# Moving small elementwise work off GpSimd in a chained attention and two-layer gated network kernel

## The chip, the cores and the metric

The kernel runs on one core of one Trainium2 chip. The metric is device time in microseconds (us), the median of several executions. A core has a matrix engine (TensorE, PE in the profile; its weight loads are PEld), VectorE (DVE), ScalarE (ACT), GpSimd (POOL) and SyncE (SP), which issues nearly all DMAs here. Each engine runs its own instructions in order.

## The reference

```python
scores = scale * (q @ k.T), causal            # q, k, v: 4 batches, 8 heads, 576 tokens, 64
local  = softmax(scores) @ v
q_p    = where(q > 0, q, exp(q) - 1) + 1
mem    = (q_p @ M_prev) / (q_p @ z_prev + 1e-6)
x      = g * mem + (1 - g) * local            # g = sigmoid(beta), per head; x: 2304 tokens x 512
xn     = x / rms(x) * rms_g
x      = (silu(xn @ w_gate) * (xn @ w_val)) @ w_out         # 512 -> 1536 -> 512
out    = (sigmoid(x @ w_gate2) * (x @ w_val2)) @ w_out2     # 512 -> 1536 -> 512
```

## The kernel before, in words

The work is cut into five **groups** of tokens. Group -1 holds the first 128 tokens of each of the four batches (512 tokens); groups 0 to 3 hold the other 448 tokens of one batch each. A group passes both gated layers, each in 12 **slices** of 128 hidden units: products with the gate and value weights (`pg`, `pv`, L1000), a tanh on ScalarE and two or three VectorE steps (`gated`), then the product with the output weights (`po`, L1066). While group g is in its layers, the attention of group g+1 is computed between its slices; so the program has an **opening** (attention of group -1 alone, written step by step in the string `ORDER`) and five stages.

Precision is kept by splitting each float32 operand into a high and a low half. For that, weights are scaled by a power of two found from a maximum. Group -1 does this for all weights, which arrive as 8-byte words: ScalarE and VectorE make float32 (`f64_top` L911, `f64_word` L917), `pair_sum` (L756) gives a sum of magnitudes per partition, `pair_scale` (L762) takes its maximum over partitions with GpSimd's `partition_all_reduce`, `two_power` (L740 to L746, VectorE) makes the scale and its inverse, ScalarE writes the scaled high half (L877) and VectorE the low half (L767). `pair_units` then lets GpSimd multiply the inverse with the token scale: `unit` and `kappa` (L775, L776) in layer 0, two columns (L778, L779) in layer 1. The tanh and the gating of the slice read those columns. The halves are saved to device memory, and later groups load them ready-made. The first two slices of layer 0 are prepared inside the opening (steps `wm`, `wp`, `wu`, `wh`, `wl` of `slice_stages`).

GpSimd's other work: maxima over partitions for the token scale `K` (L307), for values (L153), for the softmax (L597) and for the scale of the tokens between the layers (`xtop`, L1232); causal masks and fills; in the opening `phi_min` (L427), `av_add` (L420), `root` (L455) and once the scaling of `g_bc` (L1536); in the last group additions of halves for a Strassen-like product (`pair_load`, L1110) and a slice of units (L1401).

The order of the rest comes from a scheduler that places each step by priority, kept in bounds by tables, each indexed by group + 1: `DUE` (so many slices before the end of a stage the next group's attention has been dealt out), `HOLD` (the slice from which dealing starts), `AFTER` (how many slices a dealt step stays behind), `BACK` (the same for the weights of group -1), and `ONE` (between which slices of group 0 the output weights are rescaled). Weight tiles of group -1 come from a ring of six, two per slice.

Of the kernel before, what the change touches and what calls it, by code (L numbers as in the profile page):

```python
# [54 lines left out]
fill3 Aa1 W0 wp0 wu0 F0 fill3 U0 Ma2 Cb1 H0 Tb2 wt2 Vm1 Ab1 L0 fill2 S3 Va1 Xa2 Em3 Ph2 Ta2 Ph3 P2 Cb2
Ca2 Ma3 wh0 Y1 Q1 Mb3 Xa3 D2 N1 Ab2 Vm2 Aa2 wl0 Xb3 W1 fill1 P3 F1 Ta3 Ca3 U1 Tb3 Va2 D3 Vm3 Cb3 H1 wo2
Aa3 wt3 L1 Ab3 Va3 wo3 Y2 Q2 v0a g0a N2 wm1 Y3 Q3 wp1 W2 N3 F2 wh1 W3 U2 F3 wu1 a0a H2 U3 wl1 L2 H3
v1a g1a L3 dd0a a1a dd1a
# [8 lines left out]
def attn_moe_moe_kernel(ctx, tc, qT, kT, qk0, v, mz, beta, w8, rms_g, outT):  # L67
# [428 lines left out]
    def slice_stages(xt, ws, hs):  # L496

        do = {}
        for f in range(2):
# [372 lines left out]
    def halve(g, l, f, raw):  # L872
# [345 lines left out]
    def halve_tokens(g, n, po, xh):  # L1218
# [375 lines left out]
```

## Time and profile before

| | us |
|---|---|
| median of 3 executions | 1228.76 |
| lowest, highest | 1228.61, 1231.05 |
| the profiled execution: time | 1227.21 |
| the profiled execution: span of its instructions | 1225.4 |

| engine | busy us | share of the span |
|---|---|---|
| PE | 1036.7 | 85% |
| DVE | 821.2 | 67% |
| ACT | 619.3 | 51% |
| POOL | 250.4 | 20% |

The profile's busy time of an engine leaves out instructions that only set something up, so an idle time can be a wait for data or for such an instruction. In the profile's answers the idle time that an engine had before an instruction stands in brackets or behind a second bar, with what ended it; "issue" means that nothing in the profile ended it. The chain of waits is followed back from the last instruction.

### The profile page before, as it was taken

The page shows a single profiled execution, that of the slowest core. Times are in us where ns is not written, and L with a number is a line of the kernel's source. Part 1 is how long each engine was busy: PE and PEld are TensorE (multiplying, and loading weights), DVE is VectorE, ACT ScalarE, POOL GpSimd, SP SyncE. Part 2 cuts the span into 40 slices and gives each one's busy share as a digit, 9 for nine tenths or more (in the row PEclk, how much of TensorE's full clock was granted, in tenths as well). Part 3 has the DMA queues.
Part 4 walks back from the last instruction along what each step waited for, and adds up shares of the span by engine and source line. Part 5 has one row for each costly group of instructions (what it writes and reads, how often), then busy time and mean ns, then how long its engine had stood idle before and what let it go on. Part 6 is the DMA issues. An engine that isn't in the chain of part 4 may idle for free.

```text
span 1225.4 us, 18759 instructions
## 1 busy us (share of the span) xinstructions
PE 1036.7 (85%) x6721; PEld 661.7 (54%) x6721; DVE 821.2 (67%) x1730; ACT 619.3 (51%) x1078; POOL 250.4 (20%) x410
## 2 busy tenths in 40 slices
PE   4644666687658789999999999999999998799898
PEld 2532333455425446667665556655556654676675
DVE  2533446597456558888875978755878775886983
ACT  2534354568446547877553656543655542343343
POOL 2220011132112202233300312210322111330410
PEclk7778787888889899999999999999999998989999
DMA  6136464477536477886778783537644334534420
GB/s 239 53 111 243 152 206 170 153 268 259 179 138 232 160 219 259 293 259 234 253 243 259 243 273 114 179 119 225 206 150 124 129 112 108 177 129 147 147 91 36
DMA packets 90464, 223.28 MB, mean 182 GB/s; under 512 B 23938, under 2 KB 35714, under 8 KB 90370
## 3 DMA queue, kind: packets, MB, share of 16 engines
q1 hardware_dynamic: 90370, 222.08, 54.3%
q8 instruction: 53, 0.87, 0.3%
q14 instruction: 41, 0.34, 0.1%
HBM read 179.57 MB, written 38.80 MB: 178 GB/s over the span
## 4 chain that ended last, share of the span: by engine, by line
PE 51%; issue 17%; DVE 16%; ACT 7%; DMA 4%; POOL 4%; POOLq 0%; ACTq 0%; DVEq 0%
PE po L1066 14%; PE pg L1000 13%; PE pv L1000 12%; PE pw L1163 4%; PE ps L245 2%; DVE w L917 2%; ACT top L911 1%; POOL rd L1110 1%; DVE sw L1128 1%; DMA ha<-x 1%; DMA wr<-half 1%; PE pm L659 1%; DVE vl L172 1%; PE pav L610 1%; PE pav L612 1%
## 5 line engine op out<-in xcount | busy, mean ns | idle before, releaser
L1000 PEld LDWEIGHTS <-ws 128*128 128x128 f16 x1032 | 102.6, 102 | 135.3 <-issue 39.3
L1066 PE MATMUL po<-h,ws 128*128 128x448 f16 (+2 forms) x552 | 132.0, 383 | 11.8 <-DVE h L1038 6.2
L1020 ACT ACTIVATE t<-pg,unit 128x448 f32<-128x448 f32 (+2 forms) x92 | 58.5, 636 | 88.3 <-PE pg L1000 88.1
L578 POOL TENSOR_SCALAR_AFFINE_SELECT sc<-sc 128x128 f32<-128x128 f32 (+1 forms) x128 | 60.0, 484 | 155.8 <-ACT sc L573 155.2
L1000 PEld LDWEIGHTS <-wr 128*128 128x128 f16 x552 | 54.3, 99 | 61.3 <-issue 14.2
L1000 PEld LDWEIGHTS <-wl 128*128 128x128 f16 x408 | 40.1, 101 | 86.1 <-issue 23.3
L1066 PE MATMUL po<-h,wr 128*128 128x448 f16 (+1 forms) x384 | 85.1, 364 | 0.2 <-ACT h L1037 0.2
L1000 PE MATMUL pg<-ha,ws 128*128 128x448 f16 (+2 forms) x252 | 60.7, 394 | 21.2 <-DVE ws L767 11.7
L740 DVE TENSOR_SCALAR pw<-wtop 128x1 int32<-128x1 int32 x22 | 3.3, 149 | 111.5 <-POOL wtop L762 111.5
L597 POOL PARTITION_ALL_REDUCE mb<-mx x32 | 55.8, 1744 | 73.6 <-DVE mx L595 41.1
L245 PE MATMUL ps<-qq,kk 128*128 128x64 f16 (+2 forms) x280 | 54.7, 304 | 17.5 <-DVE s L746 8.1
L1066 PEld LDWEIGHTS po<-h,ws 128*128 128x128 f32 x300 | 56.4, 192 | 20.3 <-DVE h L1038 7.0
L1066 PE MATMUL po<-h,wl 128*128 128x448 f16 (+2 forms) x276 | 65.6, 381 | 0.0
L573 ACT COPY sc<-ps 128x512 f32<-128x512 f32 (+1 forms) x96 | 51.7, 559 | 20.4 <-PE ps L245 20.2
L1000 PE MATMUL pv<-hb,ws 128*128 128x448 f16 (+1 forms) x240 | 55.7, 381 | 6.5 <-DVE t L1029 4.5
L239 DVE TENSOR_TENSOR pt<-sc,pt 128x1472 f16<-128x1472 f32 x32 | 55.1, 1721 | 5.0 <-ACT pt L238 4.8
L1000 PE MATMUL pg<-hb,ws 128*128 128x448 f16 (+1 forms) x240 | 53.7, 366 | 2.0 <-ACT ws L877 1.1
L1000 PE MATMUL pv<-ha,ws 128*128 128x448 f16 (+2 forms) x252 | 54.4, 363 | 0.0
L598 DVE TENSOR_TENSOR sc<-sc,mb 128x896 f32<-128x896 f32 x32 | 34.7, 1085 | 28.3 <-POOL mb L597 28.3
L1029 DVE SCALAR_TENSOR_TENSOR t<-t,pv 128x448 f32<-128x448 f32 (+1 forms) x52 | 32.7, 629 | 28.8 <-PE pv L1000 25.1
L235 ACT ACTIVATE sc<-sc,qs 128x1472 f32<-128x1472 f32 x24 | 36.5, 1523 | 29.5 <-DVE sc L603 23.9
L1022 DVE SCALAR_TENSOR_TENSOR t<-t,pg 128x448 f32<-128x448 f32 (+2 forms) x50 | 30.8, 616 | 25.7 <-ACT t L1020 25.7
(364 smaller groups left out, 2642.2 us busy)
## 6 DMA issues: line engine op xcount, KB each, us to landing
raw<-in_w SPq DMA_DIRECT2D x22, 1023.8 KB, 5.5
ws<-half SPq DMA_DIRECT2D x34, 512.0 KB, 4.2
wr<-half SPq DMA_DIRECT2D x31, 512.0 KB, 4.3
rawl<-in_w SPq DMA_DIRECT2D x24, 511.8 KB, 6.3
wr<-parts SPq DMA_DIRECT2D x23, 512.0 KB, 5.9
ws<-parts SPq DMA_DIRECT2D x20, 512.0 KB, 5.0
kd<-in_kT SPq DMA_DIRECT2D x64, 144.0 KB, 3.7
parts<-ws SPq DMA_DIRECT2D x17, 512.0 KB, 2.9
```

The lines of the kernel that those rows point to most:

```text
L235: nc.scalar.activation(out=sc, in_=sc, func=AF.Exp, scale=both)
L239: nc.vector.tensor_tensor(out=pt[:, 1, 64:SW], in0=sc, in1=pt[:, 0, 64:SW], op=ALU.subtract)
L245: nc.tensor.matmul(ps[:, c0:c0 + n], kk[:, k0:k0 + 128], r[:, q0 - 128:q0 - 128 + n], start=(i == 0), stop=(i == 1))
L573: nc.scalar.copy(out=sc[:, o:o + c], in_=ps[:, 0:c])
L578: nc.gpsimd.affine_select(out=d, in_=d, compare_op=ALU.is_ge, fill=NEG, base=SQ[kt] - T0[kt], pattern=[[1, n]], channel_multiplier=-1,)
L597: nc.gpsimd.partition_all_reduce(mb[:, 0:448], mx[:, 0:448], channels=128, reduce_op=bass_isa.ReduceOp.max)
L598: nc.vector.tensor_tensor(out=two, in0=two, in1=mb[:, None, 0:448].to_broadcast([128, 2, 448]), op=ALU.subtract)
L1000: nc.tensor.matmul(ps[:, 0:n], w[:, a, k * 128:(k + 1) * 128], x[b][:, k, o:o + n], start=(i == 0), stop=(i == 3 * KD - 1))
L1020: nc.scalar.activation(out=t, in_=pg[:, 0:n], func=AF.Tanh, scale=u if half else 0.5)
L1029: nc.vector.scalar_tensor_tensor(out=t, in0=t, scalar=1.0, in1=pv[:, 0:n], op0=ALU.add, op1=ALU.mult)
L1066: nc.tensor.matmul(po[d][:, 0:n], w[2][:, a, c], hh[:, b, 0:n], start=(first and i == 0), stop=(last and i == 2))
L1163: nc.tensor.matmul(regions[m][at], left(i, m, a, k), right(j, b, k), start=first and c == 0, stop=c == 5, skip_group_check=True,)
```

## The change

GpSimd keeps its maxima over partitions and the masks. `pair_units` goes to ScalarE (two activations a slice in layer 0, one in layer 1, where the inverse is written straight into its column by VectorE), and so does the scaling of `g_bc`. Four maxima over partitions leave GpSimd: `K`, those of the two slices prepared in the opening, and the last group's `xtop`. In their place TensorE multiplies the column, spread over 128 columns, with the identity, and VectorE takes the maximum along the row (`widest`). `ORDER` gets two steps `wq` for that and sets `wp` and `wu` later; `K` comes first, and its load before the first load of queries and keys. The tables change.

```diff
-ONE = (1, 23, 5, 1)
-DUE = (5, 3, 3, 13, 8)
-HOLD = (1, 1, 1, 1, 1)
-BACK = (3,)
-AFTER = (1, 3, 3, 3)
+ONE = (1, 21, 6, 1)
+DUE = (6, 8, 4, 14, 8)
+HOLD = (1, 1, 1, 3, 1)
+BACK = (6,)
+AFTER = (2, 3, 2, 3)
...
-    LOADS = "q0 c q1 w0 v0 m0 b q2 v1 m1 g w1 v2 m2 q3 v3 m3 w2 w3"
+    LOADS = "c q0 q1 w0 v0 m0 b q2 v1 m1 g w1 v2 m2 q3 v3 m3 w2 w3"
...
-            top = ap_.tile([128, 1], F32, tag="gtop", name="gtop")
-            nc.gpsimd.partition_all_reduce(top, gm, channels=128, reduce_op=bass_isa.ReduceOp.max)
-            z["sx"], inv = two_power(top, 1, 7)
+            bank = zps.tile([128, 512], F32, tag="pm", name="pk")
+            z["sx"], inv = two_power(widest(gm, bank[:, 0:128])(), 1, 7)
...
+            def spread(f=f):
+                bank = z["pg", 0] if f else z["pm"][:, 0]
+                z["max", f] = widest(z["sum", f], bank[:, 384:512])
...
-                z["sw", f], z["isw", f] = pair_scale(z["sum", f])
+                z["sw", f], z["isw", f] = two_power(z["max", f](), 1, 12)
...
         if l == 0:
-            nc.gpsimd.tensor_scalar(out=unit[0][:, c], in0=inv, scalar1=half_isx, scalar2=None, op0=ALU.mult)
-            nc.gpsimd.tensor_tensor(out=kappa[:, c], in0=unit[0][:, c], in1=unit[0][:, c], op=ALU.mult)
+            nc.scalar.activation(out=unit[0][:, c], in_=inv, func=AF.Copy, scale=half_isx)
+            nc.scalar.activation(out=kappa[:, c], in_=inv, func=AF.Square, scale=half_isx)
         else:
-            nc.gpsimd.tensor_scalar(out=unit[1][:, c], in0=inv, scalar1=1.0, scalar2=None, op0=ALU.mult)
-            nc.gpsimd.tensor_scalar(out=unit[2][:, c], in0=inv, scalar1=st["half_is1"], scalar2=None, op0=ALU.mult)
+            nc.scalar.activation(out=unit[2][:, c], in_=inv, func=AF.Copy, scale=st["half_is1"])
+
+    def widest(m, bank):
+
+        nc.tensor.matmul(bank, m.to_broadcast([128, 128]), ident, start=True, stop=True)
+
+        def most():
+            top = ap_.tile([128, 1], F32, tag="wide", bufs=2, name="wide")
+            nc.vector.tensor_reduce(out=top, in_=bank, op=ALU.max, axis=AX.X)
+            return top
+
+        return most
...
-        top = ap_.tile([128, 1], F32, tag="xtop", name="xtop")
-        nc.gpsimd.partition_all_reduce(top, m, channels=128, reduce_op=bass_isa.ReduceOp.max)
+        if g == B - 1:
+            top = widest(m, late["ps"].tile([128, 512], F32, tag="pa", name="pt")[:, 0:128])()
+        else:
+            top = ap_.tile([128, 1], F32, tag="xtop", name="xtop")
+            nc.gpsimd.partition_all_reduce(top, m, channels=128, reduce_op=bass_isa.ReduceOp.max)
...
-                nc.gpsimd.tensor_scalar(out=g_bc, in0=g_bc, scalar1=z["sx"], scalar2=None, op0=ALU.mult)
+                nc.scalar.activation(out=g_bc, in_=g_bc, func=AF.Copy, scale=z["sx"])
```

How the change moves instructions shows on three engines. First GpSimd at the end of the opening and at the first slices that stage -1 prepares (`wtop` is the maximum of a weight pair's sums, `amx` that of the values, `sc` the scores of a head). An `ISA` row without operands sets up GpSimd for another kind of instruction. Before:

```order
L762 ISA
L762 ISA wtop<-sums 128x1
L775 ISA
L775 TENSOR_SCALAR unit_122<-inv,half_isx 128x1
L776 TENSOR_TENSOR kappa<-unit_122 128x1
L762 ISA
L762 ISA wtop<-sums 128x1
L775 ISA
```

And with the change:

```order
L454 TENSOR_TENSOR ri<-ss,half_neg 128x1 x2
L766 ISA
L766 ISA wtop<-sums 128x1 x4
L153 ISA amx<-am 128x1
L581 AFFINE_SELECT sc<-sc 128x64
L591 MEMSET sc 64x64
L581 AFFINE_SELECT sc<-sc 128x128
L766 ISA wtop<-sums 128x1
```

The two set-up rows that every slice had are gone. One is left behind the opening's last `root` (L454), and GpSimd has 5 such rows in the whole program where it had 51.

Second VectorE at the start of the opening, from the reduction of `rms_g` (`gm`) to the first maxima of scores (`m`, read from the score banks `ps`). Before:

```order
L305 TENSOR_REDUCE gm<-g_143 128x1
L740 TENSOR_SCALAR pw<-gtop 128x1
L742 TENSOR_SCALAR inv<-pw 128x1
L746 RECIPROCAL s_201<-inv 128x1
L309 TENSOR_SCALAR half_isx<-inv 128x1
L343 TENSOR_REDUCE m_223<-ps_181 128x4
```

With the change:

```order
L305 TENSOR_REDUCE gm<-g_141 128x1
L790 TENSOR_REDUCE wide<-pk 128x1
L743 TENSOR_SCALAR pw<-wide 128x1
L746 TENSOR_SCALAR inv<-pw 128x1
L750 RECIPROCAL s_191<-inv 128x1
L308 TENSOR_SCALAR half_isx<-inv 128x1
L342 TENSOR_REDUCE m_225<-ps_194 128x4
```

The maxima of the scores still stand behind the token scale, which now waits for TensorE (`pk`) where it waited for GpSimd (`gtop`).

Third ScalarE at the first slices of stage -1 (`top` is the first step of a weight, `sums` the measure, `ws<-w_…,s_…` the scaled half). Before:

```order
L756 ACTIVATE ws,sums<-w_707 128x2x512
L911 ACTIVATE top_133<-raw 128x1024
L716 ACTIVATE ws<-w 128x512
L911 ACTIVATE top_135<-rawl 128x512
L877 ACTIVATE ws<-w_707,s_719 128x2x512
L756 ACTIVATE wl,sums<-w_791 128x2x512
```

With the change:

```order
L760 ACTIVATE ws,sums<-w_711 128x2x512
L925 ACTIVATE top_133<-raw 128x1024
L719 ACTIVATE ws<-w 128x512
L925 ACTIVATE top_135<-rawl 128x512
L779 ACTIVATE unit_122<-inv,half_isx 128x1
L780 ACTIVATE kappa<-inv,half_isx 128x1
L891 ACTIVATE ws<-w_711,s_723 128x2x512
L760 ACTIVATE wl,sums<-w_795 128x2x512
```

The two new activations stand just ahead of the scaled half; the measure and the other steps keep their places.

## Rows read from the trace of the kernel before

**Rows 1.** Stretches from 0 to the end; x is a count of instructions.
```profile
core 0: us, PE busy (x) PEld busy (x) DVE busy (x) ACT busy (x) POOL busy (x), PEclk, DMA share, GB/s
0.00:89.00 89.00, 45.28 (x292) 34.50 (x293) 33.84 (x80) 34.01 (x106) 21.79 (x31) 0.73 0.36 130
89.00:457.00 368.00, 254.31 (x1320) 149.38 (x1318) 210.88 (x421) 193.12 (x295) 59.22 (x121) 0.84 0.58 197
457.00:640.00 183.00, 181.53 (x1248) 123.99 (x1247) 150.57 (x365) 125.98 (x233) 47.27 (x84) 1.00 0.76 260
640.00:850.00 210.00, 206.19 (x1390) 121.41 (x1390) 146.00 (x326) 104.76 (x176) 36.10 (x73) 0.99 0.65 203
850.00:1020.00 170.00, 169.78 (x1212) 101.21 (x1210) 132.48 (x275) 86.15 (x130) 40.83 (x69) 1.00 0.49 153
```

**Rows 2.** Timeline of POOL: start us, us, instruction, idle before and its releaser.
```profile
115.42 0.38 POOL L762 PARTITION_ALL_REDUCE wtop<-sums  x1 [6.11 <-issue]
123.27 0.30 POOL L775 TENSOR_SCALAR unit<-inv,half_isx 128x1 f32<-128x1 f32 x1 [7.47 <-issue]
...
130.94 0.38 POOL L762 PARTITION_ALL_REDUCE wtop<-sums  x1 [7.09 <-issue]
...
163.48 0.30 POOL L578 TENSOR_SCALAR_AFFINE_SELECT sc<-sc 128x64 f32<-128x64 f32 x1
...
165.14 0.34 POOL L762 PARTITION_ALL_REDUCE wtop<-sums  x1
```

**Rows 3.** POOL's groups in 89 to 457: busy us, mean ns, idle before.
```profile
L762 POOL PARTITION_ALL_REDUCE wtop<-sums x20 | 7.9, 393 | 100.7 <-issue 70.3 <-ACT t L1020 13.2 <-ACT ws L756 10.7
...
L775 POOL TENSOR_SCALAR unit<-inv,half_isx 128x1 f32<-128x1 f32 x10 | 4.6, 463 | 75.7 <-issue 32.7 <-DVE w L917 7.7 <-DVE am L151 7.5
L778 POOL TENSOR_SCALAR unit<-inv 128x1 f32<-128x1 f32 x10 | 4.1, 407 | 63.7 <-DVE r L637 20.5 <-issue 14.7 <-DVE ws L717 7.4
```

**Rows 4.** The chain of waits, 0 to 457: start us, us, what.
```profile
19.05 7.08 issue
...
39.01 4.53 issue
...
66.56 8.20 issue
...
75.77 6.34 issue
...
102.32 6.41 issue
...
426.63 6.61 issue
```

**Rows 5.** Timeline of DVE in the opening, the token scale.
```profile
14.03 0.15 DVE L740 TENSOR_SCALAR pw<-gtop 128x1 int32<-128x1 int32 x1 [9.30 <-POOL gtop L307]
```

**Rows 6.** Small instructions: a group of ACT; PE's timeline, four transposes.
```profile
L301 ACT ACTIVATE igate<-pb 128x8 f32<-128x8 f32 x2 | 0.3, 192 | 0.0
...
33.26 0.66 PE L364 MATMUL ps<-ident,s 128*128 128x128 f32 x4
```

**Rows 7.** Between the layers of the last group: timelines of POOL and PE.
```profile
1139.76 0.38 POOL L1232 PARTITION_ALL_REDUCE xtop<-am  x1 [36.32 <-DVE am L1230]
1148.62 0.30 POOL L1401 TENSOR_SCALAR unit<-unit,inv 128x4 f32<-128x4 f32 x1 [8.47 <-DVE tw L1089]
...
1164.69 1.67 PE L1066 MATMUL po<-h,ws 128*128 128x448 f16 x8 [3.40 <-DVE h L1045]
```

**Rows 8.** Timeline of PE where group 1 begins.
```profile
651.16 3.98 PE L1000 MATMUL pg<-ha,wr 128*128 128x448 f16 x12 [2.92 <-issue]
```

**Rows 9.** The chain of waits, 136 to 145: the products of one slice.
```profile
136.55 2.59 PE pv L1000 x12
139.14 2.80 PE po L1066 x12
141.94 2.62 PE pg L1000 x12
```

More of the change, by code (lines that the diff above doesn't have):

```diff
@@ L52 @@
 ORDER = """
-S0 K S1 fill4 G0 E0 Ma0 wt0 E1 Em0 Xa0 fill2 Ta0 Mb0 Em1 G1 Ph0 Xb0 P0 Ca0 wo0 E2 fill2 Tb0 Cb0 Ma1
+K S0 S1 fill4 G0 E0 Ma0 wt0 E1 Em0 Xa0 fill2 Ta0 Mb0 Em1 G1 Ph0 Xb0 P0 Ca0 wo0 E2 fill2 Tb0 Cb0 Ma1
 Mb1 G Xa1 Aa0 fill1 Ab0 wt1 S2 D0 Vm0 Va0 Xb1 Em2 Ph1 wo1 Ta1 Mb2 Y0 Q0 N0 P1 Tb1 Ca1 wm0 D1 E3 Xb2
[L55 to L58, printed above, removed]
+fill3 Aa1 W0 F0 fill3 U0 wq0 Ma2 Cb1 H0 Tb2 wt2 Vm1 Ab1 L0 fill2 S3 Va1 wp0 Xa2 Em3 Ph2 Ta2 Ph3 P2 Cb2
+wu0 Ca2 Ma3 wh0 Y1 Q1 Mb3 Xa3 D2 N1 Ab2 Vm2 Aa2 wl0 Xb3 W1 fill1 P3 F1 Ta3 Ca3 U1 Tb3 Va2 D3 Vm3 Cb3 H1 wo2
+Aa3 wt3 L1 Ab3 Va3 wo3 Y2 Q2 v0a g0a N2 wm1 wq1 Y3 Q3 W2 F2 U2 wp1 N3 H2 W3 wh1 F3 U3 L2 wl1 H3
+wu1 v1a g1a a0a L3 dd0a a1a dd1a
 """
@@ L295, in gates_sum @@
         def gates_sum():
-            z["bt"] = zps.tile([128, H], F32, tag="pm", name="pb")
-            nc.tensor.matmul(z["bt"], ones, bt, start=True, stop=True)
+            z["bt"] = zps.tile([128, 512], F32, tag="pm", name="pb")
+            nc.tensor.matmul(z["bt"][:, 0:H], ones, bt, start=True, stop=True)
         def gates_exp():
             for t, sign in ((igate, -1.0), (igate1, 1.0)):
-                nc.scalar.activation(out=t, in_=z["bt"], func=AF.Exp, scale=sign)
+                nc.scalar.activation(out=t, in_=z["bt"][:, 0:H], func=AF.Exp, scale=sign)
         def token_scale():
@@ L527, in lo @@
                 save_pair(0, f, both)
-            do.update({f"wm{f}": measure, f"wp{f}": power_, f"wu{f}": units, f"wh{f}": hi, f"wl{f}": lo})
+            do.update({f"wm{f}": measure, f"wq{f}": spread, f"wp{f}": power_, f"wu{f}": units, f"wh{f}": hi, f"wl{f}": lo})
             def banks(f):
@@ L734, in slot, with two_power @@
         return late["w"].tile(shape, dt, tag="rawl", bufs=NRAWL, name="wrl")
-    def two_power(m, n, top, low=-100):
+    def two_power(m, n, top, low=-100, inv=None):
         t = ap_.tile([128, n], I32, tag="pw", bufs=3, name="pw")
         nc.vector.tensor_scalar(out=t, in0=m.bitcast(I32), scalar1=0x7F800000, scalar2=None, op0=ALU.bitwise_and)
-        inv = ap_.tile([128, n], F32, tag="inv", bufs=3, name="inv")
+        if inv is None:
+            inv = ap_.tile([128, n], F32, tag="inv", bufs=3, name="inv")
         nc.vector.tensor_scalar(
@@ L757, in pair_sum, with pair_scale @@
         return sums
-    def pair_scale(sums):
+    def pair_scale(sums, inv=None):
         top = ap_.tile([128, 1], F32, tag="wtop", bufs=3, name="wtop")
         nc.gpsimd.partition_all_reduce(top, sums, channels=128, reduce_op=bass_isa.ReduceOp.max)
-        return two_power(top, 1, 12)
+        return two_power(top, 1, 12, inv=inv)
     def pair_low(raw, s, pair):
@@ L875, in halve @@
         pair = slot(g, F16)
-        s, inv = pair_scale(pair_sum(raw, pair))
+        s, inv = pair_scale(pair_sum(raw, pair), unit[1][:, f:f + 1] if l else None)
         nc.scalar.activation(out=pair[:, :, 0], in_=raw, func=AF.Copy, scale=s)
```

## The prediction, made before the changed kernel had run

> **What bounds the kernel now.** I read the engines' busy time by stretches first, with cuts at the first product of slice 0 (89 us) and at the first output stores, the end of stage -1 (457 us). From 457 us on TensorE is nearly full: busy 181.5 us of 183, 206.2 of 210, 169.8 of 170, at a granted clock of 0.99 to 1.00, the upper of its two levels, 2.4 GHz [rows 1]. Before that nothing that counts as work is full: in 89 to 457 TensorE is busy 254.3 us of 368, VectorE 210.9, ScalarE 193.1, GpSimd 59.2, and the DMAs move 197 GB/s where the next stage gets 260 [rows 1]. Something that is not work bounds 457 us of a run of 1227.
>
> GpSimd's timeline names it. A maximum over partitions takes 0.38 us, the unit after it 0.30, and each has 6 to 7.5 us of idle time before it that "issue" ends [rows 2]: maximum at 115.42, unit at 123.27, next maximum at 130.94, so a slice in 15.5 us. The idle time stands where the order has an `ISA` row, a change between maxima and elementwise work. It doesn't stand where a mask (L578) follows a maximum or a maximum follows a mask: 163.48 and 165.14 have none [rows 2]. By groups, in 89 to 457, the idle time before `wtop` is 100.7 us, before the two kinds of unit 75.7 and 63.7: 240.1 [rows 3]. With 59.2 us of work [rows 1] GpSimd is taken for 299 of 368 us, without the set-ups of the softmax maxima: it is the bound, by its set-ups.
>
> The chain of waits says how much of that lies on the path. Its pieces called "issue" of over 2 us are 5 in the opening, from 19.05 to 75.77, together 28.8 us (7.08, 4.53, 8.20 and 6.34 are shown), and 21 from 102.32 to 426.63, together 95.0 [rows 4]. All but a few, of 2 to 3 us, end at a GpSimd instruction behind a set-up. The first set-up lies ahead of the chain's first link: VectorE stands 9.30 us for `gtop` [rows 5], and every maximum of scores is queued behind that.
>
> **The change part by part.** I sum against the profiled execution (1227.21 us; the median of three is 1.55 higher). About 0.2% is what a measurement of this kernel can tell from no change.
>
> *Opening.* All of its set-ups but one go: 28.8 us of chain, and the 9.3 for `K`, in whose place stand one product of 128 columns (four take 0.66 [rows 6]) and a small reduction, with two hand-overs about 1.0. That is 37.1. The set-up left stands between the last `root` and the first slice's maximum; in the trace that `root` starts at 82.11, where the chain's last piece of the opening ends [rows 4], and the slices' maxima come after slice 0's start at 89, so the two slices made in the opening cover its 7 us; without that cover it would cost 7. Moving `K` ahead of the scores puts TensorE's first scores behind a 2 KB load, which is now issued first, ahead of 512 KB: nothing, as the warm-up products run until 5 us anyway. What is late next is the weights and inputs of the fourth batch. I take 34, with bounds 22 (that set-up bare, and 8 us lost to later loads) and 37.
>
> *Slices of stage -1.* 95.0 us of chain go, so 368 cannot fall below 273 unless the order does more. Other floors: TensorE 254 at a mean clock of 0.84; the DMAs, whose 72.5 MB (368 us at 197 GB/s) take 279 us at the 260 GB/s that stage 0 sustains [rows 1]. Of these the DMA's floor binds. I take 290 us, 11 above it, because four engines now hand to each other with 70 to 88% load each: a gain of 78. Bounds: 105 (263, TensorE's floor and 9 us of hand-overs) and 45 (323, a DMA rate of 225 GB/s, between stage 0's 260 and stage 1's 203 [rows 1]).
>
> *What the slices get in return.* 35 activations on ScalarE (24 + 10 units and `g_bc`) at about 0.19 us, as for a column of eight [rows 6]: 6.7 us, in a stretch where ScalarE would be busy 200 of 290. They stand just ahead of the scaled half. If that half were always late they would cost 22 x 0.4 = 8.4 us; I take 0, as the weights are a slice ahead.
>
> *Group 0 to 1.* Here TensorE stands 2.92 us for the tokens and then does twelve products in 3.98 us [rows 8], where twelve wider ones take 2.62 at the full clock [rows 9]; `DUE` deals attention out eight slices before the end, not three. I take 3 (0 to 5). Elsewhere in stages 0 to 2 there is nothing to gain on a full TensorE; denser dealing (stage 2 from slice 3 to 10 in place of 1 to 11) has room in VectorE, 132 of 170 us [rows 1]. I take 0 (a loss of 6 at worst).
>
> *Last group.* The maximum itself was not held up by its set-up (it waited for VectorE), but 8.47 us pass before the unit after it, and the sums for the next product are queued behind that; TensorE then stands 3.40 us [rows 7]. With no set-up there I take 3 (0 to 8). The product in the maximum's place costs about what 0.38 us on GpSimd did.
>
> **Sum**: 34 + 78 + 3 + 3 = 118; 1227.2 - 118 = 1109, and against the median **1111 us**.
>
> Two places where the Trainium skill says something else. The row: a maximum over partitions takes GpSimd 0.38 us, and it is its neighbours that cost 7 [rows 2]. The Trainium skill, GPSIMD Engine Reference, Engine selection, would have every reduction along the partitions on GpSimd. By that rule four maxima should stay there; while elementwise steps stand around them in the opening this would give back 9.3, 4.5 and 8.2 us of set-ups [rows 4, 5], a sum of 1133. This trace speaks against the rule at these places.
>
> The row: no whole stage moves more than 260 GB/s [rows 1]. The Trainium skill, DMA: Bandwidth & Descriptors, Specifications, gives about 358 GB/s as a core's share of device memory; by that the 72.5 MB would take an estimated 203 us, the DMAs would be no floor, and the case of TensorE below would be the likelier. No stage of this trace shows that rate.
>
> **The rivals.**
>
> *The transfers bind early (0.15).* Eight-byte weights go through two buffers a kind, so a load waits for VectorE to free one, and the rate may not reach stage 0's. At 231 GB/s, midway between 203 and 260, 72.5 MB take 314 us: the slices gain 54, the opening 30, the rest 4, in all 88: 1141. For it: 203 GB/s in stage 1. Against it: there TensorE was full and nothing asked for more.
>
> *TensorE binds (0.09).* If the stage gets as dense as those after it, it ends near TensorE's 254 us: 113 saved, with 37 and 7 elsewhere 157: 1072. For it: the stages after show that the program can be that dense. Against it: there the weights come ready-made.
>
> *The lookahead turns on itself: slower (0.04).* `BACK` 6 lets the weights of a slice be placed six slices ahead, but the ring of six tiles holds three slices. ScalarE's measure writes into that tile; if it is queued ahead of a tanh that frees the tile, ScalarE, and TensorE with it, waits for up to a slice's products: 2.59 + 2.80 + 2.62 = 8.0 us [rows 9]. It decides from 118 / 22 = 5.4 us a slice; at 6 us the 22 slices lose 132, and the run takes 1243. Against it: in ScalarE's order the measure keeps its place among the slices.
>
> *The set-ups stay (0.03).* If maxima and masks needed set-ups that no row of the order shows, the idle time before `wtop` would remain: 1227, within 0.2%. Against it: the two instructions without idle time [rows 2].
>
> **How the numbers follow.** 0.69 for the forecast, whose own range is 1085 to 1140, and the rivals as given. Faster: 0.69 + 0.15 + 0.09 = 0.93; within 0.2%: 0.03; slower: 0.04. The range leaves out the slow and the empty case and about half of TensorE's: 1078 at the lower end (a gain of 150, opening and slices near their upper bounds); at the upper 1162, all lower bounds at once (22 + 45 + 0 + 0 = 67).
>
> **What would show it.** In the new profile the slices' maxima follow each other without the 7 us; VectorE waits for `wtop` under 15 us in all; slice 0 begins at 50 to 60 us, not 89; the first output stores come near 345, not 457, with TensorE busy over 80% in between and the DMAs near 250 GB/s. From there the stages are as long as before within a few us. I am wrong if the first stage ends after 390, if VectorE or ScalarE waits in it for a weight tile for several us a slice, or if stages 0 to 2 grow by over 10 us together.

## The result and the profile after

The changed kernel takes 1051.09 us, the median of four runs (1050.46 to 1053.93), against 1228.68 for the kernel before (four runs, 1225.12 to 1231.05): a ratio of 0.8561 with a 95% interval of 0.8535 to 0.8588. That is 177.6 us less where 118 less was forecast, and it lies below the range's lower end of 1078. The profiled execution took 1050.51 us, its span 1048.7.

The page of the changed kernel: busy time and share by engine, the clock by fortieths of the span, the DMAs' mean, and the shares of the chain of waits.

```profile
PE 1002.3 (96%) x6729; PEld 647.7 (62%) x6729; DVE 820.2 (78%) x1734; ACT 625.4 (60%) x1113; POOL 242.6 (23%) x361
...
PEclk9999999999999999999999999999999899899999
...
DMA packets 90463, 223.28 MB, mean 213 GB/s; under 512 B 23938, under 2 KB 35714, under 8 KB 90370
...
PE 49%; DVE 12%; DMA 5%; ACT 4%; issue 3%; POOL 3%; SPq 0%; POOLq 0%; ACTq 0%; DVEq 0%
```

The bytes are the same as before (223.28 MB), TensorE is busy for 96% of the span, and "issue" is down to 3% of the chain, from 17%.

The stretches say where the time came from. The cuts are the first product of slice 0 (46.9 us, where it was 89.1), the first output stores (279.1, where they were 456.9), and then each group's first stores. The columns are those of [rows 1]. First the kernel before, cut by these marks, then the changed one.

```profile
0.00:89.10 89.10, 45.38 (x293) 34.59 (x294) 33.84 (x80) 34.11 (x106) 21.79 (x31) 0.73 0.36 130
89.10:456.90 367.80, 254.11 (x1318) 149.23 (x1317) 210.78 (x421) 193.02 (x295) 59.22 (x121) 0.84 0.58 197
456.90:657.50 200.60, 196.21 (x1315) 133.13 (x1314) 157.29 (x379) 131.11 (x242) 47.88 (x85) 0.99 0.78 261
657.50:848.10 190.60, 189.71 (x1315) 111.35 (x1314) 139.02 (x312) 99.62 (x167) 35.48 (x72) 1.00 0.61 196
848.10:1045.10 197.00, 190.94 (x1319) 112.33 (x1317) 145.24 (x293) 92.29 (x140) 44.46 (x71) 0.98 0.45 142
1045.10:1220.20 175.10, 159.90 (x1170) 121.04 (x1169) 134.18 (x248) 68.14 (x129) 41.57 (x30) 0.97 0.34 117
```

```profile
0.00:46.90 46.90, 40.60 (x299) 30.29 (x300) 34.62 (x84) 34.81 (x111) 17.13 (x23) 0.96 0.69 254
46.90:279.10 232.20, 221.84 (x1312) 138.68 (x1311) 208.67 (x419) 196.29 (x323) 56.94 (x81) 0.99 0.88 309
279.10:479.60 200.50, 197.12 (x1321) 133.76 (x1320) 156.73 (x385) 133.56 (x246) 51.37 (x86) 0.99 0.79 263
479.60:668.80 189.20, 188.92 (x1314) 111.06 (x1314) 138.35 (x306) 99.09 (x163) 35.54 (x71) 1.00 0.63 198
668.80:868.00 199.20, 190.97 (x1314) 111.53 (x1313) 147.23 (x293) 93.01 (x141) 43.72 (x71) 0.98 0.45 141
868.00:1043.40 175.40, 162.40 (x1177) 122.34 (x1175) 133.75 (x249) 67.72 (x128) 37.87 (x29) 0.96 0.35 117
```

The opening gave 42.2 us, the slices of stage -1 gave 135.6 (367.8 to 232.2), and everything behind them lost 1.1: 176.7 of span. In the slices about the same products (1,312 in the record, 1,318 before) keep TensorE busy for 221.8 us at a granted clock of 0.99, where they took 254.1 at 0.84, and the DMAs move 309 GB/s, not 197.

GpSimd's timeline, against [rows 2]: a maximum over partitions behind a mask or behind the memory fill of L591 has no idle time or waits for ScalarE's sum, and in the slices no row's idle time ends with "issue".

```profile
102.61 0.14 POOL L591 MEMSET sc<- 64x64 f32 x1
102.71 1.10 POOL L581 TENSOR_SCALAR_AFFINE_SELECT sc<-sc 128x128 f32<-128x128 f32 x1
103.79 0.35 POOL L766 PARTITION_ALL_REDUCE wtop<-sums  x1
106.32 2.38 POOL L581 TENSOR_SCALAR_AFFINE_SELECT sc<-sc 128x128 f32<-128x128 f32 x2 [2.18 <-ACT sc L576]
111.88 0.94 POOL L766 PARTITION_ALL_REDUCE wtop<-sums  x1 [3.18 <-ACT wl L760]
```

Among VectorE's waits in the slices (us in total, times, longest), `wtop` is down from 93.3 us to 1.8, before and after:

```profile
DVE pw L740 <- POOL wtop L762: 93.3, 14, 13.5
```

```profile
DVE pw L743 <- POOL wtop L766: 1.8, 4, 1.1
```

In the opening VectorE makes the token scale from 6.13 us on, not from 14.03 behind 9.30 us of waiting [rows 5]:

```profile
5.80 0.29 DVE L790 TENSOR_REDUCE wide<-pk 128x1 f32<-128x128 f32 x1 [2.94 <-PE pk L786]
6.13 0.15 DVE L743 TENSOR_SCALAR pw<-wide 128x1 int32<-128x1 int32 x1
```

### The profile page after: what moved, and what is told of

Read it like the earlier page. It is cut to its first block, busy times and chain, and to the rows that moved or that the text cites. A ratio compares the mean times of both kernels' runs of the same rounds, so it can differ in the third digit from the quotient of the medians.

```text
span 1048.7 us, 18670 instructions
## 1 busy us (share of the span) xinstructions
PE 1002.3 (96%) x6729; PEld 647.7 (62%) x6729; DVE 820.2 (78%) x1734; ACT 625.4 (60%) x1113; POOL 242.6 (23%) x361
## 2 busy tenths in 40 slices
DMA packets 90463, 223.28 MB, mean 213 GB/s; under 512 B 23938, under 2 KB 35714, under 8 KB 90370
## 4 chain that ended last, share of the span: by engine, by line
PE 49%; DVE 12%; DMA 5%; ACT 4%; issue 3%; POOL 3%; SPq 0%; POOLq 0%; ACTq 0%; DVEq 0%
PE po L1080 15%; PE pg L1014 13%; PE pv L1014 12%; PE pw L1177 4%; PE ps L245 2%; POOL rd L1124 2%; DVE sw L1142 1%; DMA wr<-half 1%; DMA out_T<-o 1%; PE pm L662 1%; DVE tw L1103 1%; DMA ha<-x 1%; PE pav L615 1%; POOL mb L600 1%; PE pav L613 1%
## 5 line engine op out<-in xcount | busy, mean ns | idle before, releaser
L1014 PEld LDWEIGHTS <-ws 128*128 128x128 f16 x1008 | 96.5, 99 | 93.0 <-issue 6.4
L1080 PE MATMUL po<-h,ws 128*128 128x448 f16 (+2 forms) x528 | 124.5, 380 | 0.7 <-DVE h L1059 0.4
L1080 PE MATMUL po<-h,wr 128*128 128x448 f16 (+1 forms) x396 | 90.2, 372 | 0.0
L1080 PE MATMUL po<-h,wl 128*128 128x448 f16 (+2 forms) x252 | 58.5, 376 | 0.9 <-ACT h L1058 0.9
L1080 PEld LDWEIGHTS po<-h,ws 128*128 128x128 f32 x276 | 52.3, 192 | 10.4 <-DVE h L1052 0.4
L1080 PE MATMUL po<-h,wrl 128*128 128x448 f16 (+1 forms) x240 | 52.9, 362 | 0.0
L1014 PE MATMUL pg<-ha,ws 128*128 128x448 f16 (+2 forms) x252 | 52.4, 355 | 0.3 <-DVE ws L771 0.3
L1014 PEld LDWEIGHTS <-wrl 128*128 128x128 f16 x336 | 32.4, 98 | 30.3 <-issue 2.3
L1014 PE MATMUL pg<-hb,ws 128*128 128x448 f16 (+1 forms) x228 | 49.3, 362 | 0.0
L1014 PE MATMUL pv<-hb,ws 128*128 128x448 f16 (+1 forms) x228 | 49.1, 361 | 0.0
```

The costliest lines, as they stand in the source:

```text
L1014: nc.tensor.matmul(ps[:, 0:n], w[:, a, k * 128:(k + 1) * 128], x[b][:, k, o:o + n], start=(i == 0), stop=(i == 3 * KD - 1))
L1080: nc.tensor.matmul(po[d][:, 0:n], w[2][:, a, c], hh[:, b, 0:n], start=(first and i == 0), stop=(last and i == 2))
```

## The experiments

Eighteen kernels ran. The table has what they measured; "first product" and "slices" are of the profiled execution, as above, and the ratio is to the kernel before on the same chip. Two things help to read it. Up to the first output stores the order of TensorE, VectorE and ScalarE is the same in the traces of the changed kernel, v1 and v2, and their slices took 232.2, 233.8 and 238.2 us: differences of under 6 us say nothing by themselves. And an edit inside the slices makes the scheduler lay out the queues anew. ScalarE's order up to the first output stores has 418 rows in the changed kernel's trace, with repeats merged; of these 6 are missing or stand elsewhere in o1, but 133 in w0, 137 in u2, 171 in w1 and 172 in d1.

| run | first product | slices | stage 0 | median us | ratio, 95% interval |
|---|---|---|---|---|---|
| before | 89.1 | 367.8 | 200.6 | 1228.68 | 1 |
| changed | 46.9 | 232.2 | 200.5 | 1051.09 | 0.8561 [0.8535, 0.8588] |
| e1_units | 88.3 | 241.5 | 198.2 | 1097.34 | 0.8935 [0.8905, 0.8964] |
| e2_units_back | 48.1 | 376.8 | 204.3 | 1199.67 | 0.9765 [0.9743, 0.9788] |
| e3_old_numbers | 46.2 | 244.3 | 201.5 | 1056.09 | 0.8595 [0.8577, 0.8613] |
| e4_new_numbers | 89.9 | 369.2 | 206.3 | 1238.13 | 1.0073 [1.0051, 1.0095] |
| o1_old_order | 45.5 | 236.5 | 200.2 | 1052.14 | 0.8573 [0.8547, 0.8599] |
| h1_layer1_units_back | 45.6 | 294.5 | 201.8 | 1111.77 | 0.905 [0.9031, 0.9069] |
| d1_more_stores | 47.8 | 237.2 | 207.1 | 1061.24 | 0.8633 [0.8584, 0.8683] |
| d2_more_stores_twice | 46.9 | 251.8 | 212.0 | 1079.29 | 0.8781 [0.8738, 0.8824] |
| p1_more_products | 46.6 | 249.1 | 197.1 | 1062.92 | 0.8648 [0.8596, 0.8699] |
| p0_fewer_products | 46.3 | 226.0 | 211.9 | 1054.85 | 0.8579 [0.8535, 0.8624] |
| u2_units_twice | 48.4 | 243.2 | 205.5 | 1065.97 | 0.8677 [0.8654, 0.8701] |
| u0_units_on_vector | 46.4 | 241.0 | 200.6 | 1057.81 | 0.8626 [0.8588, 0.8665] |
| w1_more_vector | 47.9 | 254.7 | 200.6 | 1076.94 | 0.8785 [0.8752, 0.8817] |
| w0_less_vector | 47.2 | 246.0 | 200.0 | 1063.43 | 0.866 [0.8631, 0.8688] |
| w0p0_less_both | 46.7 | 226.1 | 207.5 | 1042.57 | 0.8484 [0.8453, 0.8516] |
| v1_first_adds_dve | 46.7 | 233.8 | 201.1 | 1048.49 | 0.8542 [0.852, 0.8564] |
| v2_all_adds_dve | 46.8 | 238.2 | 201.5 | 1030.87 | 0.8404 [0.838, 0.8427] |
| v3_adds_units_vector | 46.3 | 241.6 | 201.8 | 1038.11 | 0.8462 [0.8438, 0.8486] |

### The parts of the change by themselves

**e1, the units alone**, on the kernel before (with `kappa`, `unit[2]` and `g_bc` in the same way, and `inv` written straight into `unit[1]`):

```diff
-            nc.gpsimd.tensor_scalar(out=unit[0][:, c], in0=inv, scalar1=half_isx, scalar2=None, op0=ALU.mult)
+            nc.scalar.activation(out=unit[0][:, c], in_=inv, func=AF.Copy, scale=half_isx)
```

> The kernel before with one part of the change: the slices' units (and g_bc) go from GpSimd to ScalarE; maxima, opening and dealing numbers stay as before. Theory 1 (the set-ups around the units were the whole bound of stage -1, and without them TensorE at the full clock is the floor): the slices take 235 to 245 us from their first product to the first output stores, not 367.8, TensorE is busy about 222 us of them at a clock of 0.97 or more, and the opening, which keeps its set-ups for three maxima, ends only some 5 to 12 us earlier: about 1085 us in all (1070 to 1095). Rival (the new dealing numbers, the lookahead of 6 above all, are needed to fill TensorE): slices of 270 to 300 us, 1110 to 1160 us.

The slices fell to 241.5 us with the old dealing numbers: the rival falls. The windows of the opening and of the slices:

```profile
0.00:88.30 88.30, 46.90 (x294) 35.81 (x295) 33.97 (x81) 35.51 (x111) 17.87 (x26) 0.71 0.36 131
88.30:329.80 241.50, 225.66 (x1318) 140.00 (x1316) 211.32 (x421) 197.65 (x324) 47.07 (x81) 0.98 0.88 302
```

My 5 to 12 us for the opening did not come (88.3 us, where it was 89.1), and the total lies just above the forecast for it. The opening's maxima stand among other elementwise work of GpSimd (`e`, `x`, `ri`), so each still needs a set-up. Three of the six in its GpSimd timeline:

```profile
42.39 0.38 POOL L763 PARTITION_ALL_REDUCE wtop<-sums  x1 [6.78 <-issue]
49.85 1.53 POOL L427 TENSOR_SCALAR e<-e 128x512 f32<-128x512 f32 x1 [7.08 <-ACT qk L369]
...
73.36 0.38 POOL L763 PARTITION_ALL_REDUCE wtop<-sums  x1 [8.98 <-issue]
```

**e2, the rest of the change without the units**: the diff above turned round, on the changed kernel.

> The changed kernel with its units and g_bc put back on GpSimd; spreads, order of the opening and dealing numbers are the new ones. Theory 1: the slices go back to about 368 us (15.5 us a slice) at a clock near 0.84, the opening keeps most of its gain of 42 us: about 1187 us (1178 to 1200). Rival (the lookahead of 6 lets GpSimd run ahead and hides part of the set-ups): slices of 330 us or less, 1150 us or less.

Theory 1 holds: first product at 48.1, slices 376.8 at a clock of 0.82. A lookahead of six slices hides nothing of the set-ups.

```profile
48.10:424.90 376.80, 255.90 (x1314) 151.94 (x1312) 210.27 (x419) 193.34 (x293) 61.28 (x121) 0.82 0.56 190
```

So moving the units carries the slices, and the maxima that left GpSimd carry the opening: e1 saved 132 us and e2 29, the whole change 178; the 17 in excess were not taken apart.

**h1, part of the dose**: the unit of layer 1 alone back on GpSimd, in 10 of the 24 slices.

```diff
-            nc.scalar.activation(out=unit[2][:, c], in_=inv, func=AF.Copy, scale=st["half_is1"])
+            nc.gpsimd.tensor_scalar(out=unit[2][:, c], in0=inv, scalar1=st["half_is1"], scalar2=None, op0=ALU.mult)
```

> The changed kernel with the units of layer 1 alone (10 slices) put back on GpSimd. Theory 1 (each slice with a unit on GpSimd costs two set-ups in series, 15.5 us a slice, whatever else is fast): the 10 slices take 155 us instead of about 94: 55 to 65 us more, 1106 to 1116 us; layer 0 (first product to the maximum of the layer's boundary, 119 us) is as before. Rival (a few set-ups hide behind TensorE's work): 10 us more or less.

Layer 1, from the maximum `xtop` to the first stores, took 170.8 us (169.3 to 340.1) in place of 113.2 (165.9 to 279.1): 57.6 for 10 slices, or 5.8 a slice. One slice in GpSimd's timeline shows the loop of 14.4 us from maximum to maximum, of which the two set-ups are 13.0; the rest is the maximum, the unit, two masks and a fill. First the window of the slices, then that loop:

```profile
45.60:340.10 294.50, 238.42 (x1306) 145.34 (x1304) 211.20 (x420) 195.50 (x314) 53.31 (x91) 0.91 0.71 243
```

```profile
204.93 0.38 POOL L766 PARTITION_ALL_REDUCE wtop<-sums  x1 [6.53 <-issue]
...
212.59 0.30 POOL L782 TENSOR_SCALAR unit<-unit,inv 128x1 f32<-128x1 f32 x1 [6.89 <-issue]
...
219.29 0.38 POOL L766 PARTITION_ALL_REDUCE wtop<-sums  x1 [6.14 <-issue]
```

**e3 and e4, the dealing numbers**: the changed kernel with the old ones, and the kernel before with the new ones.

```diff
-ONE = (1, 21, 6, 1)
-DUE = (6, 8, 4, 14, 8)
-HOLD = (1, 1, 1, 3, 1)
-BACK = (6,)
-AFTER = (2, 3, 2, 3)
+ONE = (1, 23, 5, 1)
+DUE = (5, 3, 3, 13, 8)
+HOLD = (1, 1, 1, 1, 1)
+BACK = (3,)
+AFTER = (1, 3, 3, 3)
```

> The changed kernel with the dealing numbers of before (ONE, DUE, HOLD, BACK, AFTER); the opening's order stays new. Theory 1 (the numbers are worth nothing by themselves, TensorE sets the pace): 1051 us within 5, slices of 230 to 236 us. Rival (a lookahead of 6 slices keeps the weights ahead, one of 3 does not): VectorE or ScalarE is late with weights by 1 us or more a slice, 1075 us or more.

> The kernel before with the changed kernel's dealing numbers alone. Theory 1 (GpSimd's set-ups bound stage -1 whatever the dealing): 1229 us within 8. Rival of the prediction (the lookahead of 6 turns on itself): 1243 us or more, with TensorE idle behind a tanh or ScalarE idle for a weight tile. Second rival (a longer lookahead overlaps the set-ups): 1215 us or less.

e3 is 5.0 us slower than the changed kernel, as theory 1 allows, but its slices are 6 to 12 us longer (244.3 for 232.2 to 238.2) and leave theory 1's range; stage 2 gives 2.6 back (196.6 against 199.2 us). e4 is 9.2 us slower than the kernel before on the same chip (1228.91), 5.7 us of it in stage 0 and 4.7 in stage 2, and only 1.4 in the slices: a little more than theory 1 allowed, and far from both rivals. The numbers cost a little in stage 2: it took 195.2 to 197.1 us in the three kernels with the old ones, and 197.6 to 201.8 in the fourteen with the new ones that leave the last group's adds on GpSimd. That they pay in the slices once GpSimd no longer sets the pace rests on e3 alone. The rival of the prediction, a lookahead that turns on itself, does not show in the slices of either kernel that has `BACK` 6.

**o1, the opening's order**: the old `ORDER` and `LOADS`, each spread just ahead of its reduction.

```diff
-K S0 S1 fill4 G0 E0 Ma0 wt0 E1 ...
+S0 K S1 fill4 G0 E0 Ma0 wt0 E1 ...
...
-    LOADS = "c q0 q1 w0 v0 m0 b q2 v1 m1 g w1 v2 m2 q3 v3 m3 w2 w3"
+    LOADS = "q0 c q1 w0 v0 m0 b q2 v1 m1 g w1 v2 m2 q3 v3 m3 w2 w3"
```

> The changed kernel with the opening's order and order of loads of before; each spread's product stands just ahead of its reduction. Theory S (the opening's gain comes from the maxima that left GpSimd, which took five set-ups with them): first product of the slices within 4 us of 46.9, 1051 to 1056 us in all. Rival (it is the order: scores behind K, spreads ahead of the queue): 5 to 15 us later, 1057 to 1067 us.

Theory S: 45.5 us and 1052.14. The order of the opening is worth nothing that can be measured. Its 42 us come from the maxima that left GpSimd: e1, without the units but with these maxima, kept 88.3 us, and e2, with the units but without them, had 48.1.

### What the slices stand on now

**d1 and d2, more traffic**: each halved pair is stored once or twice more.

```diff
         nc.sync.dma_start(out=parts[l, f], in_=pair)
+        for i in range(1):
+            extra = dp.tile([128, 2, 2, 512], F16, name="extra_%d_%d_%d" % (l, f, i))
+            nc.sync.dma_start(out=extra, in_=pair)
```

> The changed kernel, and each of the 24 halved pairs of weights is stored once more to a place that nobody reads (0.52 MB each; 11 to 12.6 MB in stage -1, 16% more). Theory T: slices within 0 to 8 us of 232 (the DMAs' share rises from 0.88 to about 1.0), 1051 to 1059 us. Theory D (309 GB/s is what the DMAs give): 11.5 MB at 309 GB/s are 37 us, 1088 us.

> The same with two more stores of each pair (23 to 25 MB, a third more). Theory T: now the DMAs must bind, 95 MB at the 386 GB/s of the fastest stretch of the changed kernel are 246 us, at 350 GB/s 271: slices of 246 to 275 us, 1065 to 1095 us; the rate of this run is the DMAs' floor here. Theory D: twice the loss of the run with one more store, slices near 306 us, 1125 us.

The slices of d1, then of d2:

```profile
47.80:285.00 237.20, 222.22 (x1304) 139.88 (x1303) 211.24 (x419) 197.40 (x323) 60.34 (x81) 0.98 0.96 344
```

```profile
46.90:298.70 251.80, 225.92 (x1304) 138.62 (x1302) 211.53 (x417) 198.79 (x321) 42.93 (x81) 0.97 0.96 359
```

With 10 MB more the slices take 5 us longer, within their scatter, and not 37; with 19 MB more the DMAs move 359 GB/s, and the slices are longer by 20 us. So 309 GB/s was what the slices asked for, not what the DMAs can give; the changed kernel's 71.7 MB at 359 GB/s would be 200 us, under TensorE's 221.8 and VectorE's 208.7 and about ScalarE's 196.3. The totals grew by 10 and 28 us (d1's a little over theory T's 1059), since stage 0 grew too (207.1 and 212.0 us); why it did is open.

**p1 and p0, more and fewer products**: two extra products ahead of each accumulation, or the third of three left out.

```diff
+                for again in range(2 if more and i == 0 else 0):
+                    nc.tensor.matmul(ps[:, 0:n], w[:, a, k * 128:(k + 1) * 128], x[b][:, k, o:o + n], start=True, stop=True)
```

```diff
-            for a, b in ((0, 0), (0, 1), (1, 0)):
+            for a, b in ((0, 0), (1, 0)) if few else ((0, 0), (0, 1), (1, 0)):
```

> The changed kernel with two more products ahead of each accumulation of the hidden layer in stage -1 (what they write is overwritten): 88 of 512 columns and 8 of 256, by 12 products in 2.62 us about 20 us of TensorE. Theory T (TensorE is the floor of the slices, at the full clock): slices of 252 us (248 to 255) instead of 232.2, 1070 us in all. Theory D (the DMAs, 309 GB/s, are the floor) or V (VectorE, busy 208.7 of 232.2 us): slices within 5 us of 232, 1051 to 1056 us.

> The changed kernel without the third of the three products (high part of the weight by low part of the token) in the hidden layer of stage -1: a part of the computation that it leaves out, 176 products of 512 columns and 16 of 256, about 40 us of TensorE. Theory T: the slices fall until the next floor, VectorE's 208.7 us of work or the DMAs: 210 to 222 us, 1029 to 1041 us in all. Theory D or V (one of these binds already): slices of 228 to 233 us, 1046 to 1052 us. Either way how far they fall prices the next floor.

p1: TensorE's work rose by 19.7 us (221.84 to 241.57), the slices by 16.9, and TensorE stood idle for 7.5 us of them:

```profile
46.60:295.70 249.10, 241.57 (x1414) 148.74 (x1412) 211.46 (x421) 198.56 (x325) 57.55 (x81) 0.99 0.86 296
```

That is theory T's for the slices; the total came 7 us under its 1070, of which stage 0 gave 3.4. p0 fits neither theory: 31 us less of TensorE, and the slices shortened by 6. Its window and the first products of stage 0, in p0 and then in the changed kernel:

```profile
46.30:272.30 226.00, 190.75 (x1112) 121.46 (x1111) 204.47 (x411) 192.81 (x317) 54.25 (x81) 0.95 0.88 311
```

```profile
283.28 4.60 PE L1014 MATMUL pg<-ha,wr 128*128 128x448 f16 x12 [10.27 <-DMA ha<-x]
```

```profile
278.13 2.43 PE L1014 MATMUL pg<-ha,wr 128*128 128x448 f16 x12 [0.90 <-DMA ha<-x]
```

What they gained came back as 10.27 us of waiting for the next group's tokens, where it was 0.90. So something else binds close under TensorE's floor.

**u2, u0, w1, w0 and w0p0** look for it on ScalarE and VectorE. u2 issues each unit's activation twice. u0 puts the units on VectorE. w1 computes half of the low parts twice. w0 leaves out one step of the gate in layer 0, and w0p0 that and p0's products:

```diff
+        nc.vector.scalar_tensor_tensor(
+            out=pair[:, 0, 1], in0=raw[:, 0], scalar=s, in1=pair[:, 0, 0], op0=ALU.mult, op1=ALU.subtract
+        )
```

```diff
-            nc.vector.scalar_tensor_tensor(out=t, in0=t, scalar=1.0, in1=pg[:, 0:n], op0=ALU.add, op1=ALU.mult)
+            if g >= 0:
+                nc.vector.scalar_tensor_tensor(out=t, in0=t, scalar=1.0, in1=pg[:, 0:n], op0=ALU.add, op1=ALU.mult)
```

(the first is w1, the second w0).

> The changed kernel with every unit's activation on ScalarE issued twice: 34 more activations of about 0.19 us, 6.5 us of ScalarE in stage -1. Theory (off the path, as the prediction had it): 1051 us within 2. Rival (they stand ahead of what TensorE waits for): 5 to 9 us more.

> The changed kernel with the units on VectorE instead of ScalarE (34 instructions of about 0.15 us, 5 us). If the units on ScalarE cost what a second set of them cost (15 us), and VectorE hides its 5 us: 1036 to 1045 us. If they cost nothing where they are, or VectorE is as tight: 1051 to 1060 us.

> The changed kernel, and VectorE computes one half of each pair's low parts twice (512 columns, 0.69 us, 22 times behind the opening: 15 us of VectorE, 209 become 224 of 232 us). Theory T (TensorE alone is the floor of the slices): slices within 3 us of 232 to 238, 1051 to 1056 us in all. Theory C (VectorE and ScalarE stand in one chain with TensorE, since a slice's weights, its tanh and its products go through all three): 8 to 15 us more, 1059 to 1066 us.

> The changed kernel without VectorE's first step of the gate in layer 0 of stage -1 (the tanh plus 1, times the gate's product; left out, 10 times 0.68 us and 2 times 0.42: 7.6 us of VectorE). Theory T (TensorE is the floor of the slices): slices of 232 to 238 us, 1051 us within 2. Theory C (VectorE is in the chain of every slice as TensorE is): slices of 226 to 231 us, 1043 to 1048 us.

> The changed kernel without that step and without the third product of the hidden layer in stage -1 (two parts of the computation left out). Theory T: as with the products alone left out, slices near 226 us, 1055 us in all. Theory C: slices of 214 to 220 us; in all 1043 to 1052 us, since with fewer products the next stage stood 10 us for its tokens, and that wait stays.

The slices of u2, w1 and w0, one fence each:

```profile
48.40:291.60 243.20, 225.20 (x1314) 140.76 (x1313) 211.28 (x420) 202.64 (x354) 60.33 (x81) 0.97 0.85 294
```

```profile
47.90:302.60 254.70, 228.19 (x1311) 140.12 (x1309) 224.00 (x440) 198.12 (x324) 55.27 (x81) 0.96 0.82 282
```

```profile
47.20:293.20 246.00, 226.47 (x1317) 140.30 (x1316) 204.97 (x408) 197.41 (x324) 52.80 (x81) 0.97 0.85 295
```

u2 adds 6.3 us of ScalarE and costs 14.9; w1 adds 15.3 of VectorE and costs 25.9. Both cost more than the recorded theory that has a cost (5 to 9 us for u2, 8 to 15 for w1). But w0 takes 3.7 us of VectorE's busy time away (204.97 for 208.67) and *costs* 12.3: neither theory allows it. u0, w0 and u2, which add and take work, lost 9, 14 and 11 us in the slices, and doses of this size can't be put down to one engine. Nor is it shown that the new layout of the queues is what costs: d1 moved as many of ScalarE's rows as w1 and lost 5 us. Only w0p0, with both reliefs, gains: 8.5 us by medians, with slices no shorter than p0's (226.1) and a wait of 6.53 us at the start of stage 0 in place of 10.27. u0 shows one more thing: with the units on VectorE the slices are as short as in e1 (241.0 and 241.5 us), so what counts is that the units left GpSimd, not which engine took them.

What stands: with the same products TensorE works 222 to 228 us, and the slices took 232 to 246 us in the eleven kernels that have these products, no unit on GpSimd and not the doses of w1 and d2. TensorE at the full clock is the largest floor. What makes up the 10 to 24 us above 222 stays open, and so does which engine comes next; the order of the queues differs between most of these kernels and is a candidate that no run isolates.

### A faster version

The changed kernel has one long set-up left on the path. From the chain of waits:

```profile
803.72 6.28 issue
810.00 4.12 POOL rd L1124 x2
814.14 3.86 DMA wl<-half
```

v1 puts the first pair's adds of the last group on VectorE, v2 all of them, v3 those and the units.

```diff
-                nc.gpsimd.tensor_tensor(out=raw[i][:, m], in0=ws[i][m][:, 0], in1=ws[i][m][:, 1], op=ALU.add)
+                nc.vector.tensor_tensor(out=raw[i][:, m], in0=ws[i][m][:, 0], in1=ws[i][m][:, 1], op=ALU.add)
```

> An attempt at a faster version: the changed kernel with the first pair of weights' adds of the last group (the ones behind its one open set-up at 803 us) on VectorE instead of GpSimd. If the 6.79 us of set-up stand on the path (TensorE then waits 5.90 us at 817.81): 3 to 7 us less, 1044 to 1048 us. If VectorE's own work takes their place: 1051 us within 2.

> As the attempt before, with all the pairs' adds of the last group on VectorE: the wait of 3.20 us for rd at 885 and VectorE's slowed sums beside GpSimd's adds (1.2 us for 0.4) go, 2.5 us of VectorE per pair come. If TensorE's gap of 5.49 us at 889.57 comes from these: 5 to 12 us less, 1040 to 1046 us. If VectorE (133 of 178 us) becomes the bound there: 1051 us or more.

> An attempt at a faster version: all the pairs' adds of the last group and the units on VectorE, so that GpSimd has no elementwise work but the opening's. If both gains add (20 us measured for the adds, 6 to 15 for the units): 1016 to 1026 us. If the units cost nothing on ScalarE: 1031 us within 4. If VectorE is as tight as ScalarE in the slices: 1035 to 1046 us.

v1 is 2.6 us faster by medians, at the edge of the scatter, though its stage 2 fell from 199.2 to 194.1 us, below the 197.6 to 201.8 of the fourteen kernels counted under e4. v2 takes 1030.87 us (five runs, 1029.32 to 1036.4), faster than both kernels and than forecast. In its profiled execution, the slowest of the five, stage 2 is 9.5 us shorter and the last group 11.4, at a granted clock of 1.00 in place of 0.96. Its last two stretches:

```profile
675.70:865.40 189.70, 188.84 (x1319) 111.22 (x1318) 146.54 (x301) 93.20 (x141) 31.00 (x63) 1.00 0.48 148
865.40:1029.40 164.00, 157.53 (x1172) 118.36 (x1170) 131.04 (x277) 68.19 (x128) 0.33 (x1) 1.00 0.39 125
```

VectorE has no more work there than before (131.0 against 133.8 us), though it took the adds over. The timelines suggest why. In the changed kernel VectorE's sums ran beside GpSimd's adds, here from 887.79 to 892.8 us, and TensorE then stood 5.49 us for VectorE; then the same work in v2, where its longest wait for VectorE between 865 and 900 us is 1.82.

```profile
887.79 2.45 POOL L1124 TENSOR_TENSOR rw<-ws 128x512 f32<-128x512 f16 x2 [1.38 <-DMA ws<-half]
...
888.13 2.39 DVE L1142 TENSOR_TENSOR sw<-rd 128x256 f32<-128x256 f32 x2
...
895.06 1.28 PE L1177 MATMUL pw<-ha,wr 128*128 128x224 f16 x6 [5.49 <-DVE cw L1225]
```

```profile
880.77 1.29 DVE L1124 TENSOR_TENSOR rd<-wr 128x512 f32<-128x512 f16 x2
...
883.70 0.41 DVE L1142 TENSOR_TENSOR sw<-rd 128x256 f32<-128x256 f32 x1
```

A sum of 256 columns takes VectorE 1.2 us beside GpSimd's adds and 0.41 without; an add takes GpSimd 1.2 us and VectorE 0.65. v3 is 7.2 us slower than v2, u0 6.7 slower than the changed kernel, and both have longer slices (241.6 and 241.0 us): nothing speaks for moving the units on from ScalarE.

## Why the prediction was right and wrong

**The bound was read rightly.** GpSimd's set-ups held up the first 457 us. e1 took the slices' set-ups away and gave 126 us there (367.8 to 241.5); e2 put them back and the slices took 376.8; h1 put ten slices' back, and GpSimd's loop was 14.4 us again.

**The step that failed** is the new length of the slices, with TensorE's floor at 254 us and the DMAs' at 279: "Of these the DMA's floor binds. I take 290 us, 11 above it". Both floors were rates of engines that something else held up. The 260 GB/s of stage 0 [rows 1] are what a full TensorE asked for; the slices now draw 309, and d2 drew 359. And "TensorE 254 at a mean clock of 0.84" is work priced at what was granted to an engine that stood still for 114 of 368 us, a mean between its two levels, 1.2 and 2.4 GHz; at 0.99, the upper level nearly throughout, the same products take 221.8. The rows of before had it: 254.3 x 0.84 = 214 us at the full clock. The margin that I put on the floor, 11 us for hand-overs, was right: 232.2 - 221.8 = 10.4. A floor of 222 with that margin gives 233 and a gain of 135; it was 135.6, and that alone is 58 of the 60 us by which the forecast was off. Some of this fit is luck: the rows of before alone give 214 + 11 = 225, and the margin was 10 to 24 us in the eleven kernels above.

A second bound of the same sum failed with it: "95.0 us of chain go, so 368 cannot fall below 273 unless the order does more". The slices ended 41 us under that. The chain's other pieces were taken at the length that they had; but TensorE's busy time alone fell by 32.3 us (254.1 to 221.8) as the granted clock rose. That these 32 are most of the 41 is a sum that fits, not a thing shown.

The Trainium skill, DMA: Bandwidth & Descriptors, Specifications, gives about 358 GB/s as a core's share of device memory. d2's slices come out there, with 359 GB/s over 252 us, but the figure is no ceiling here: the changed kernel moved 386 from 75 to 100 us. The prediction weighed the figure and set it aside, because no whole stage showed it; a short stretch of the kernel before did, 389 GB/s from 651.2 to 655.1 us. First that stretch, then the changed kernel's:

```profile
651.20:655.10 3.90, 3.90 (x13) 1.63 (x14) 0.00 (x0) 0.00 (x0) 0.00 (x0) 0.60 1.03 389
```

```profile
75.00:100.00 25.00, 22.74 (x101) 13.00 (x100) 24.49 (x49) 22.25 (x38) 6.03 (x9) 0.93 1.01 386
```

**Opening**: 34 forecast, bounds 22 to 37, 42.2 measured. The chain's 37.1 are in it; TensorE's busy time there fell by 4.8 us besides (45.38 to 40.60, the clock from 0.73 to 0.96), a term that the sum did not have. That the two make up the 42.2 is a sum that fits, not a thing shown. o1 confirms that moving `K` costs and brings nothing that can be measured.

**Units on ScalarE**: sized at 0.19 us, they take 0.28 to 0.32. Whether they cost anything where they stand was not settled: twice as many cost 14.9 us, but so did less work elsewhere.

**Group 0 to 1 and last group**, 3 and 3: nothing net. TensorE's gap of 2.92 us [rows 8] is gone and the one of 3.40 [rows 7] is down to 0.38, with 2.11 us on another operand 4 us later; yet the stages are as long as before within 2.1 us.

**Stages 0 to 2**, 0 with a loss of 6 at worst: right, though by e3 and e4 the new numbers cost stage 2 some 3 to 5 us.

**The rivals.** That TensorE binds (0.09, 1072) was the nearest case, with the wrong price, 254 us in place of 222, and p0 shows that it does not bind alone. That the transfers bind early falls with d1 and d2. That the set-ups stay falls with the timeline of the slices above. That the lookahead turns on itself falls with the changed kernel's own slices; e4 is slower by 0.73%, but in other stages. By the rule that reductions over partitions belong on GpSimd (the Trainium skill, GPSIMD Engine Reference, Engine selection) the four maxima would have stayed: e1 has three of them where they were in the opening, and its first product comes at 88.3 us, not 46.9. At these places the measurement decides against the rule; the fourth, the last group's, no run tested by itself.

## What to carry to other kernels

A floor is a rate times an amount, and a rate read in a stage that something else holds up is no floor: scale TensorE's busy time by the clock granted in the stretch before you compare it, and take a DMA rate from a stretch only if its DMAs, not an engine, were what it waited for. When the old bound goes and several engines come within 10% of each other, expect small edits to move the time by some per cent either way, and test a small idea there against the scatter that edits of the other sign bring too. On GpSimd count the changes between maxima over partitions and elementwise work, not the work: in h1 a unit of 0.3 us kept GpSimd's loop at 14.4 us, and each slice was 5.8 us longer.

## What the runs showed of the hardware

- In the kernel before, GpSimd changed 44 times between maxima over partitions and elementwise work in the first 457 us; the idle time ahead of the first instruction after each change was 5.9 to 10.8 us, 329 us in all, waits for data included. Between maxima and masks no such time stands (163.48 and 165.14 us, [rows 2]).
- The granted clock went with the idle time: about the same 1,310 products took 255.9 us at 0.82 (e2), 238.4 at 0.91 (h1) and 221.8 at 0.99; busy time times clock is 210 to 220 us in all three.
- The DMAs' busy share does not say what is left: 0.96 went with 344 GB/s in d1 and with 359 in d2.
- VectorE's sum of two sources beside GpSimd's adds took three times as long as alone (1.2 us for 0.41), and with the adds moved to VectorE its own total in the last group was no larger (131.0 us for 133.8).
